# A fused attention and MLP kernel: exps of q and k moved behind the logits' exp, VectorE's steps spread between matmuls, logits spaced differently

## Chip, cores and metric

The kernel runs on 1 core of one Trainium2 chip. The metric is the device time in microseconds (us) of one execution; each figure for a kernel is the median over repeated runs. A core has several engines, each with its own queue of instructions that it executes in order: TensorE (PE in the profile, its weight loads PEld), VectorE (DVE), ScalarE (ACT), GpSimd (POOL) and SyncE (SP, which here only issues DMAs). They wait for one another through semaphores. Matmul results go to PSUM, which has 8 banks; SBUF is the other on-chip memory.

## What is computed

From `x` (2048 tokens of width 1024, bfloat16) the layer-normalised `xn` is formed, and the output is `x + A(xn) + B(xn)`. `B` is an MLP over the token axis. `A` is attention of 32 heads of 32 columns, over 4 segments of 512 tokens, with a memory that each segment leaves for the next:

```python
phi = lambda t: jnp.where(t > 0, t + 1.0, jnp.exp(t))
g = _sigmoid(beta).reshape(1, H, 1, 1)
for s in range(N):
    logits = jnp.einsum('bhqd,bhkd->bhqk', qs, ks) * scale + mask
    p = _softmax(logits, axis=-1)
    a_dot = jnp.einsum('bhqk,bhkd->bhqd', p, vs)
    pq = phi(qs)
    num = jnp.einsum('bhld,bhde->bhle', pq, M)
    den = jnp.einsum('bhld,bhd->bhl', pq, z)[..., None] + 1e-06
    o = g * (num / den) + (1.0 - g) * a_dot
    pk = phi(ks)
    M = M + jnp.einsum('bhld,bhle->bhde', pk, vs)
    z = z + jnp.einsum('bhld->bhd', pk)
return o @ wo
```

The mask is causal within a segment, and `phi(t)` is computed as `max(t + 1, min(exp(t), 1))`.

## The kernel before

The MLP runs first, up to about 352 us, then attention. All instructions are issued by one Python program, in the order in which its functions are called; each engine executes its own in that order, and a small framework adds the semaphore waits. Nothing reorders them afterwards.

**Units.** Attention is cut into 32 units, one for each group of four heads in each segment: unit `u` is segment `u // 8`, group `u % 8`. The loop of `attention` (L1313) runs over the units.

**Dense work.** The projections are jobs of 8 matmuls of 128x512 each, kept in the queue `self.jobs` and run in order by `dense(n)`, which issues the next `n` of these matmuls, across job borders. A job uses PSUM bank 6 or 7, in turn, and when its eighth matmul has been issued its `end` issues what empties the bank: a ScalarE copy into `qT` (`q_job`) or `vA` (`v_job`), a VectorE copy into `kT` (`k_job`), or a VectorE addition into `fin` (`wo_job`, the output projection). The bank can be written again once that is done. In unit `u` the queue holds the output projections planned for it, one v job up to unit 27, and the q and k jobs of unit `u + 2` up to unit 29. So units 10 to 25 and 27 have four jobs (32 matmuls, in the order wo, v, q, k), unit 30 has two (wo, wo), unit 31 three (wo), and the others three: v, q, k in units 0 to 9 and 26, wo, q, k in units 28 and 29.

**Logits.** `logits(u, step)` multiplies q and k of four heads at once into banks 0 to 3 and then issues one ScalarE exp over all four banks into `pT`, and one GpSimd select for each diagonal block, which zeroes what the mask excludes. Step 0 is the first block of rows of k, step 1 the second and the fourth; step 2, the third, is done for two units together in the even one. The next logits can be written when the exp has read the banks.

**Weighing.** `weigh(u - 1, part)` multiplies `pT` with v, phi(q) with the memory, and in part 2, in segments 0 to 2, phi(k) with v for the memory's update. Parts 0 and 2 write bank 4, part 1 bank 5. After each part VectorE copies the result into `ost`; after part 2 it also updates the memory (`MZ`, `MZbf`, L1254 to L1258). Part 2 can start only when the copy of part 0 has emptied bank 4.

**Mixing and phi.** `combine(u - 1)` is VectorE's mixing of the two attention results: three small operations for the scales (`srec`, L1282 to L1284), the product `prod` (L1285), and the addition into `o_s` (L1289). In segment 0 there is no memory and it has two small operations and one product. `phi_q` and `phi_k` are two VectorE operations each (L1070 and L1072), on an exp that ScalarE has put into one of the four buffers `etmp` before; that exp is issued by the `end` of the q or k job. `k_transpose` sends phi(k) through a transposing DMA into `pk`; `o_transpose_dma` does so for `o_s`. In the first four units of segments 0 to 2 a chunk of `x` for the next segment is loaded (`xn_load`), scaled on VectorE (`xn_scale`) and transposed (`xn_transpose`).

**Order in a unit.** `cut` divides the unit's matmuls among five stretches by shares. An even unit issues logits 0, 6 dense matmuls, weighing parts 0 and 1, 2 dense, weighing part 2, phi of k, the scaling of x, 4 dense, logits 1, combine, phi of q, 12 dense, logits 2, and 8 dense (shares of 32; with 24 they are 4, 2, 3, 9 and 6). An odd unit issues 4 dense, logits 0, 6 dense, weighing parts 0 and 1, 2 dense, weighing part 2, phi of k, the scaling, 6 dense, logits 1, combine, phi of q, and 14 dense. After the last unit `tail` finishes the last segment's output.

In the profile, every matmul has line L198, that of a helper, so one tells them by the names of their tiles: `ps_all<-qT,kT` are logits; `vA,pT`, `MZbf,pqT` and `vA,pk` are weighing; `xnT,wq`, `xnT,wk`, `wv,xnT` and `wo,oT` are dense.

Of the kernel before, what the change touches and what calls it, by code (L numbers as in the profile page):

```python
# [6 lines left out]
ACT = mybir.ActivationFunctionType  # L7
# [12 lines left out]
P = 128  # L20
# [364 lines left out]
class _Kernel:  # L385
# [678 lines left out]


    def phi(self, dst, R_dst, src, R_src, k, u):

        fw = self.fw
        et, R_et, mt = self.etmp[2 * (u % 2) + k], self.R_etmp[2 * (u % 2) + k], self.mtmp[k]
        fw.op("dve", lambda e: e.tensor_scalar(mt[:], et[:], 1.0, None, op0=ALU.min),  # L1070
              reads=[R_et], writes=[self.R_mtmp[k]])
        fw.op("dve", lambda e: e.scalar_tensor_tensor(dst, src, 1.0, mt[:], op0=ALU.add, op1=ALU.max),  # L1072
              reads=[R_src, self.R_mtmp[k]], writes=[R_dst])
# [16 lines left out]
    def q_job(self, u):  # L1090
        def end(b):
            fw, k = self.fw, u % 3
            fw.op("act", lambda e: e.activation(self.qT[k][:], self.bank(b), ACT.Copy),  # L1093
                  reads=[self.R_bank[b]], writes=[self.R_qT[k]])
            if u >= N_GRP:
                fw.op("act", lambda e: e.activation(self.etmp[2 * (u % 2)][:], self.qT[k][:], ACT.Exp),  # L1096
                      reads=[self.R_qT[k]], writes=[self.R_etmp[2 * (u % 2)]])
        return self.proj_job(self.wq_ring, u, end)

    def k_job(self, u):  # L1100
        def end(b):
            fw, k = self.fw, u % 3
            fw.op("dve", lambda e: e.tensor_copy(self.kT[k][:], self.bank(b)),  # L1103
                  reads=[self.R_bank[b]], writes=[self.R_kT[k]])
            if u // N_GRP < N_SEG - 1:
                fw.op("act", lambda e: e.activation(self.etmp[2 * (u % 2) + 1][:], self.kT[k][:], ACT.Exp),  # L1106
                      reads=[self.R_kT[k]], writes=[self.R_etmp[2 * (u % 2) + 1]])
        return self.proj_job(self.wk_ring, u, end)
# [151 lines left out]

    def combine(self, u):
        fw = self.fw
        s, g, o = u // N_GRP, u % N_GRP, u % 2
        ost, R_ost = self.ost[o], self.R_ost[o]
        rec, R_rec = self.srec[:, o, :], self.R_srec[o]
        os, R_os = self.o_s[o], self.R_os[o]
        if s == 0:
# [3 lines left out]
            fw.op("dve", lambda e: e.tensor_tensor(rv, rv, self.gate[:, g, None, 0, :].to_broadcast([P, 4, 4]),  # L1271
                                                   op=ALU.mult), reads=[R_rec, self.R_gate], writes=[R_rec])
            fw.op("dve", lambda e: e.tensor_tensor(os[:].rearrange("p q (r d) -> p q r d", d=D_HEAD),
                                                   v[:, :, 0, :, 0:D_HEAD],
                                                   rv.unsqueeze(3).to_broadcast([P, 4, 4, D_HEAD]), op=ALU.mult),
                  reads=R_ost + [R_rec], writes=[R_os])
            return
        sums = ost[:, :, D_HEAD].rearrange("p (q a) -> p q a", q=4)
        rv = rec.rearrange("p (q a) -> p q a", q=4)
        e8 = self.eps8[:].rearrange("p k r -> p (k r)")[:, None, :].to_broadcast([P, 4, 8])  # L1280
        g8 = self.gate[:, g, :, :].rearrange("p k r -> p (k r)")[:, None, :].to_broadcast([P, 4, 8])
        fw.op("dve", lambda e: e.tensor_tensor(rv, sums, e8, op=ALU.add), reads=R_ost + [self.R_eps8], writes=[R_rec])  # L1282
        fw.op("dve", lambda e: e.reciprocal(rec, rec), reads=[R_rec], writes=[R_rec])
        fw.op("dve", lambda e: e.tensor_tensor(rv, rv, g8, op=ALU.mult), reads=[R_rec, self.R_gate], writes=[R_rec])  # L1284
        fw.op("dve", lambda e: e.tensor_tensor(self.prod[:], ost[:, :, 0:D_HEAD],  # L1285
                                               rec.unsqueeze(2).to_broadcast([P, 32, D_HEAD]), op=ALU.mult),
              reads=R_ost + [R_rec], writes=[self.R_prod])
        pv = self.prod[:].rearrange("p (q k r) d -> p q k (r d)", q=4, k=2)
        fw.op("dve", lambda e: e.tensor_tensor(os[:], pv[:, :, 0, :], pv[:, :, 1, :], op=ALU.add),  # L1289
              reads=[self.R_prod], writes=[R_os])  # L1290

# [15 lines left out]

    WO_FIRST = 10

# [9 lines left out]
    def attention(self):  # L1319
        self.jobs, self.turn = deque(), 0  # L1320
        self.wo_plan = {}
        for s in range(N_SEG - 1):
# [3 lines left out]
        self.jobs.extend([self.q_job(0), self.k_job(0)] + [self.v_job(0, c) for c in range(4)])  # L1326
        self.dense(16)
        self.phi_k(0)
        self.k_transpose(0)
# [4 lines left out]
        for u in range(N_UNIT):  # L1334
# [17 lines left out]
            self.dense(cuts[1] if not even else 0)  # L1352
            if u:
# [32 lines left out]
    def tail(self):  # L1386
# [30 lines left out]
        self.weigh(u, 2)  # L1417
        self.combine(u)
        product(3, 0, 6)
# [38 lines left out]
```

## Time and profile before

| what | value |
|---|---|
| median of 11 runs | 666.29 us (665.48 to 668.38) |
| device time of the profiled execution | 667.29 us |
| its span (first to last instruction) | 665.5 us |
| granted TensorE clock | 1.00 throughout |

Stretches of the profiled execution, from the view that gives busy time by window:

| stretch, us | what | long | TensorE busy | VectorE | ScalarE | GpSimd |
|---|---|---|---|---|---|---|
| 0 to 365.5 | MLP, first projections | 365.5 | 361.89 | 198.65 | 76.12 | 53.01 |
| 365.5 to 442.7 | units 0 to 9 | 77.2 | 75.39 | 45.19 | 63.58 | 25.43 |
| 442.7 to 598.1 | units 10 to 25 | 155.4 | 152.69 | 131.96 | 109.17 | 49.64 |
| 598.1 to 649.9 | units 26 to 31 | 51.8 | 48.55 | 37.80 | 33.45 | 16.76 |
| 649.9 to 665.5 | tail | 15.6 | 12.93 | 8.88 | 0.60 | 0.00 |

A row of a timeline gives the start in us from the span's start, the busy time, the engine, the line, the operation with its tiles, the number of instructions merged into the row, and in brackets the idle time before it with what ended it. A row of the chain of waits gives start, length, and the engine with its tile and line. A matmul's busy time includes its way through the array, so rows of TensorE overlap, and a TensorE that is busy all the time can still issue matmuls later than it could. DMA transfers land, in the median, 2.3 us after issue for `pk`, 3.7 us for `oT`, 3.2 us for `xnT`, and 3.4 and 3.9 us for a group's `wq` and `wk`.

### The profile page before, as it was taken

The numbers are of one execution on the slowest core, as the hardware profiler recorded it, in microseconds if no ns is written. First come the engines' busy times: TensorE is split into PE (matmuls) and PEld (weight loads), VectorE is DVE, ScalarE is ACT, GpSimd is POOL, SyncE is SP. The second block draws the span as 40 slices with busy tenths as digits, with TensorE's granted clock in tenths as the row PEclk, the third lists the DMA queues.
The fourth block names the chain that finished last, engine by engine and source line by source line (L and its number), as shares of the span: only waits on it lengthen the run. The fifth ranks groups of instructions, "written<-read, shape, count | busy, mean of one in ns | idle before, by whom it ended". The sixth has DMA issues, their size and how long they took to land.

```text
span 665.5 us, 11075 instructions
## 1 busy us (share of the span) xinstructions
PE 651.4 (98%) x4622; PEld 301.6 (45%) x4622; DVE 422.5 (63%) x789; ACT 282.9 (43%) x305; POOL 144.8 (22%) x181
## 2 busy tenths in 40 slices
PE   8999999999999999999999999989999999999988
PEld 3444444444444444444444444444444444444434
DVE  6965676665653554335442455588889988776775
ACT  7442232322300000000012888866767666767750
POOL 2500000000020222202250333333332233323330
PEclk9999999999999999999999999999999999999999
DMA  9704242242637644665185686586446765434225
GB/s 309 198 0 128 64 123 67 68 123 64 178 122 205 159 142 126 175 175 142 67 222 176 162 177 118 112 158 153 111 120 125 167 146 120 119 88 77 75 75 134
DMA packets 187241, 87.64 MB, mean 132 GB/s; under 512 B 116024, under 2 KB 174392, under 8 KB 187192
## 3 DMA queue, kind: packets, MB, share of 16 engines
q1 hardware_dynamic: 187048, 86.91, 51.9%
q8 instruction: 36, 0.59, 0.4%
q14 instruction: 13, 0.11, 0.1%
q10 hardware_dynamic: 144, 0.03, 0.0%
HBM read 67.13 MB, written 8.39 MB: 113 GB/s over the span
## 4 chain that ended last, share of the span: by engine, by line
PE 81%; ACT 9%; DVE 7%; issue 1%; DMA 1%; SPq 0%; DVEq 0%
PE ps_all L198 81%; ACT pT L1198 6%; ACT etmp L1096 1%; DVE prod L1285 1%; ACT qT L1093 1%; DVE mtmp L1070 1%; DMA xin<-in_A_x_dram 1%; DVE o_s L1289 1%; DVE kT L1103 1%; ACT etmp L1106 1%; DVE gate L558 1%; DVE fin L1406 1%; DVE ost L1248 1%; DVE mtmp L1072 1%; DVE pqT L1072 0%
## 5 line engine op out<-in xcount | busy, mean ns | idle before, releaser
L1198 ACT ACTIVATE pT<-ps_all 128x2048 bf16<-128x2048 f32 x80 | 149.6, 1869 | 29.6 <-PE ps_all L198 29.5
L1202 POOL TENSOR_SCALAR_AFFINE_SELECT pT<-pT 128x512 bf16<-128x512 bf16 x128 | 91.8, 734 | 209.5 <-ACT pT L1198 209.5
L690 DVE TENSOR_TENSOR part<-ps_all,part 128x512 f32<-128x512 f32 x76 | 55.5, 730 | 117.1 <-PE ps_all L198 116.2
L926 POOL TENSOR_TENSOR part<-part,stg 128x512 f32<-128x512 f32 x24 | 33.0, 1402 | 265.0 <-DVE part L690 248.1
L695 ACT ACTIVATE part<-ps_all 128x512 f32<-128x512 f32 x20 | 11.9, 597 | 149.0 <-PE ps_all L198 149.0
L742 ACT ACTIVATE g<-part,b1c 128x512 f16<-128x512 f32 x36 | 26.0, 722 | 98.8 <-DVE part L690 98.8
L198 PE MATMUL ps_all<-wv,xnT 128*128 128x512 bf16 x256 | 66.8, 379 | 0.0
L198 PE MATMUL ps_all<-wo,oT 128*128 128x512 bf16 (+2 forms) x272 | 64.2, 367 | 1.4 <-DVE fin L1146 1.3
L198 PE MATMUL ps_all<-xnT,wq 128*128 128x512 bf16 x256 | 65.2, 380 | 0.0
L1248 DVE CAST ost<-ps_all 128x396 bf16<-128x396 f32 (+2 forms) x96 | 42.8, 474 | 33.3 <-PE ps_all L198 32.5
L198 PE MATMUL ps_all<-xnT,wk 128*128 128x512 bf16 x256 | 61.8, 380 | 0.0
L198 PE MATMUL ps_all<-g,sum 128*128 128x512 f16 x224 | 51.0, 379 | 0.8 <-DVE part L690 0.8
L198 PEld LDWEIGHTS ps_all<-vA,pT 128*128 128x128 bf16 x1280 | 42.2, 96 | 19.7 <-DVE ost L1248 10.5
L198 PE MATMUL ps_all<-g,w2s 128*128 128x512 f16 x224 | 51.0, 379 | 0.0
L198 PE MATMUL ps_all<-gT,sum 128*128 128x512 f16 x224 | 49.7, 379 | 0.0
L198 PE MATMUL ps_all<-vA,pT 128*128 128x33 bf16 x1280 | 45.2, 178 | 1.6 <-DVE ost L1248 1.6
L198 PE MATMUL ps_all<-h,sum 128*128 128x512 f16 x192 | 45.2, 379 | 0.0
L198 PE MATMUL ps_all<-h,w1s 128*128 128x512 f16 x192 | 44.9, 379 | 0.0
L198 PE MATMUL ps_all<-hT,sum 128*128 128x512 f16 x192 | 43.6, 379 | 0.0
L198 PEld LDWEIGHTS ps_all<-xnT,wk 128*128 128x128 bf16 x256 | 23.8, 98 | 29.9 <-issue 3.2
L198 PE MATMUL ps_all<-qT,kT 32*128 32x384 bf16 (+3 forms) x512 | 31.7, 301 | 4.8 <-ACT pT L1198 3.9
L198 PEld LDWEIGHTS ps_all<-wo,oT 128*128 128x128 bf16 x272 | 23.2, 97 | 27.5 <-issue 5.8
(98 smaller groups left out, 817.9 us busy)
## 6 DMA issues: line engine op xcount, KB each, us to landing
w2s<-in_B_w_dram SPq DMA_DIRECT2D x8, 1792.0 KB, 8.5
w1s<-in_B_w_dram SPq DMA_DIRECT2D x12, 1024.0 KB, 5.6
wq<-in_A_wq_dram SPq DMA_DIRECT2D x32, 256.0 KB, 3.4
wk<-in_A_wk_dram SPq DMA_DIRECT2D x32, 256.0 KB, 3.9
stg<-in_A_x_dram SPq DMA_DIRECT2D x16, 256.0 KB, 2.9
xs<-in_A_x_dram SPq DMA_DIRECT2D x16, 256.0 KB, 4.2
out_dram<-stg SPq DMA_DIRECT2D x16, 256.0 KB, 2.8
fin<-out_dram SPq DMA_DIRECT2D x16, 256.0 KB, 3.1
```

Of the source, the lines that this page charges most:

```text
L198: ins = self.nc.tensor.matmul(*args, **kwargs)
L558: fw.op("dve", lambda e: e.tensor_copy(self.gate[:, :, 1, :], gv), reads=[self.R_gcol, self.R_gate], writes=[self.R_gate])
L690: self.fw.op("dve", lambda e: e.tensor_tensor(self.tmp[dst][:], self.bank(b), self.tmp[src][:], op=ALU.add), reads=[self.R_bank[b], self.R ...
L695: self.fw.op("act", lambda e: e.activation(self.tmp[dst][:], self.bank(b), ACT.Copy), reads=[self.R_bank[b]], writes=[self.R_tmp[dst]])
L742: self.fw.op("act", lambda e: e.activation(self.gB[f % 2][half][:, f // 2, :], src, ACT.Gelu_apprx_tanh, bias=self.b1c[:, f:f + 1], scale= ...
L926: fw.op("pool", lambda e: e.tensor_tensor(self.tmp[t][:], self.tmp[t][:], self.stg[k][:, 512 * half:512 * half + 512], op=ALU.add), reads= ...
L1070: fw.op("dve", lambda e: e.tensor_scalar(mt[:], et[:], 1.0, None, op0=ALU.min), reads=[R_et], writes=[self.R_mtmp[k]])
L1072: fw.op("dve", lambda e: e.scalar_tensor_tensor(dst, src, 1.0, mt[:], op0=ALU.add, op1=ALU.max), reads=[R_src, self.R_mtmp[k]], writes=[R_ ...
L1093: fw.op("act", lambda e: e.activation(self.qT[k][:], self.bank(b), ACT.Copy), reads=[self.R_bank[b]], writes=[self.R_qT[k]])
L1198: fw.op("act", lambda e: e.activation(dst, src, ACT.Exp, scale=SCALE), reads=self.R_bank[0:4], writes=[R[v % 2][kb] for v, kb, _ in blocks ...
L1202: fw.op("pool", lambda e: e.affine_select(d, d, pattern=[[0, 4], [1, P]], compare_op=ALU.is_ge, fill=0.0, base=0, channel_multiplier=-1), ...
L1248: fw.op("dve", lambda e: e.tensor_copy(dst, src), reads=[self.R_bank[b]], writes=[self.R_ost[o][part]])
```

## The change

Three things are changed in the attention phase; nothing is computed differently.

- The exps of q and k are no longer issued at the end of their jobs. They are noted in `self.exps`, and `late_exps`, called at the end of `logits`, issues them behind that logits' exp and its selects.
- `combine` returns its work as a list of steps (two in segment 0, else four, with the product in two halves), and these steps, phi of q, phi of k with its transpose, and the scaling with its transpose are put into a queue `self.side`. `dense` takes one step from it after every three matmuls. Phi of q is now that of unit `u` in unit `u`, not that of `u + 1`. What is left at the unit's end is issued there.
- The shares are now 5, 1, 3, 15, 8 in an even unit (logits 0, 5 dense, weighing parts 0 and 1, 1 dense, part 2, 3 dense, logits 1, 15 dense, logits 2, 8 dense) and 7, 4, 1, 4, 16 in an odd one (7 dense, logits 0, 4 dense, parts 0 and 1, 1 dense, part 2, 4 dense, logits 1, 16 dense).

```diff
+    def late_exps(self):
+        for k, src, R, u in self.exps:
+            n = 2 * (u % 2) + k
+            assert self.in_etmp[n] is None, (n, u, self.in_etmp)
+            self.in_etmp[n] = u
+            self.fw.op("act", lambda e: e.activation(self.etmp[n][:], src[:], ACT.Exp), reads=[R], writes=[self.R_etmp[n]])
+        self.exps = []
...
             if u >= N_GRP:
-                fw.op("act", lambda e: e.activation(self.etmp[2 * (u % 2)][:], self.qT[k][:], ACT.Exp),
-                      reads=[self.R_qT[k]], writes=[self.R_etmp[2 * (u % 2)]])
+                self.exps.append((0, self.qT[k], self.R_qT[k], u))
...
             if u // N_GRP < N_SEG - 1:
-                fw.op("act", lambda e: e.activation(self.etmp[2 * (u % 2) + 1][:], self.kT[k][:], ACT.Exp),
-                      reads=[self.R_kT[k]], writes=[self.R_etmp[2 * (u % 2) + 1]])
+                self.exps.append((1, self.kT[k], self.R_kT[k], u))
...
             stop = min(at + n, 8)
+            if self.side:
+                stop = min(stop, at + max(1, self.SIDE_EVERY - self.since))
...
             if stop == 8:
                 end(b)
                 self.jobs.popleft()
+            self.since += stop - at
+            if self.side and self.since >= self.SIDE_EVERY:
+                self.side.popleft()()
+                self.since = 0
...
+        self.late_exps()
...
+        def products(half):
+            n = slice(16 * half, 16 * half + 16)
+            fw.op("dve", lambda e: e.tensor_tensor(self.prod[:, n, :], ost[:, n, 0:D_HEAD],
+                                                   rec[:, n].unsqueeze(2).to_broadcast([P, 16, D_HEAD]), op=ALU.mult),
+                  reads=R_ost + [R_rec, self.R_prod], writes=[self.R_prod])
...
+        if s == 0:
+            return [scales_first, products_first]
+        return [scales, lambda: products(0), lambda: products(1), add]
...
-    WO_FIRST = 10
+    SIDE_EVERY = 3
...
+            cuts = self.cut(total, (5, 1, 3, 15, 8) if even else (7, 4, 1, 4, 16))
             if even:
-                cuts = (self.cut(total, (6, 2, 4, 12, 8)))
                 self.logits(u, 0)
             else:
-                cuts = (self.cut(total, (4, 6, 2, 6, 14)))
-            self.dense(cuts[0])
-            if not even:
+                self.dense(cuts[0])
                 self.logits(u, 0)
             if u > 1:
                 self.o_transpose_dma(u - 2)
-            self.dense(cuts[1] if not even else 0)
+            self.dense(cuts[0] if even else cuts[1])
             if u:
                 self.weigh(u - 1, 0)
                 self.weigh(u - 1, 1)
             self.dense(cuts[1] if even else cuts[2])
             if u:
                 self.weigh(u - 1, 2)
+                steps = self.combine(u - 1)
+                self.side.append(steps.pop(0))
+            if N_GRP <= u:
+                self.side.append(lambda: self.phi_q(u))
+            if u:
+                self.side.extend(steps)
             if u + 1 < N_UNIT:
-                self.phi_k(u + 1)
-                self.k_transpose(u + 1)
+                self.side.append(lambda: (self.phi_k(u + 1), self.k_transpose(u + 1)))
             if xn:
-                self.xn_scale(c)
+                self.side.append(lambda: (self.xn_scale(c), self.xn_transpose(c)))
             self.dense(cuts[2] if even else cuts[3])
             self.logits(u, 1)
-            if u:
-                self.combine(u - 1)
-            self.phi_q(u + 1)
-            if xn:
-                self.xn_transpose(c)
             if even:
                 self.dense(cuts[3])
                 self.logits(u, 2)
             self.dense(100)
+            while self.side:
+                self.side.popleft()()
```

In the changed program's order on VectorE, a unit of segments 1 to 3 has the three copies into `ost`, the memory's update, the scales, phi of q, both halves of `prod`, the addition into `o_s`, phi of k, the scaling of x where there is one, and the copy into `kT`; an even unit's `fin` stands right behind the scales, an odd unit's ahead of the copies. Before, `fin` of an even unit stood between the second and the third copy.

More of the change, by code (lines that the diff above doesn't have):

```diff
@@ L1063, in before_attention @@
                       reads=[self.R_diag], writes=[self.R_diag])
+    def late_exps(self):
[5 more added lines that the diff above has]
+        self.exps = []
     def phi(self, dst, R_dst, src, R_src, k, u):
         fw = self.fw
+        assert self.in_etmp[2 * (u % 2) + k] == u
+        self.in_etmp[2 * (u % 2) + k] = None
         et, R_et, mt = self.etmp[2 * (u % 2) + k], self.R_etmp[2 * (u % 2) + k], self.mtmp[k]
@@ L1266, in combine, with scales_first @@
         os, R_os = self.o_s[o], self.R_os[o]
-        if s == 0:
+        def scales_first():
             v = ost[:].rearrange("p (q k r) x -> p q k r x", q=4, k=2)
@@ L1272, in combine, with products_first @@
                                                    op=ALU.mult), reads=[R_rec, self.R_gate], writes=[R_rec])
+        def products_first():
+            v = ost[:].rearrange("p (q k r) x -> p q k r x", q=4, k=2)
+            rv = rec[:, 0:16].rearrange("p (q r) -> p q r", q=4)
             fw.op("dve", lambda e: e.tensor_tensor(os[:].rearrange("p q (r d) -> p q r d", d=D_HEAD),
@@ L1276, in combine @@
                   reads=R_ost + [R_rec], writes=[R_os])
[L1277 to L1288, printed above, removed]
@@ L1289, in combine, with scales @@
-        fw.op("dve", lambda e: e.tensor_tensor(os[:], pv[:, :, 0, :], pv[:, :, 1, :], op=ALU.add),
-              reads=[self.R_prod], writes=[R_os])
+        def scales():
+            sums = ost[:, :, D_HEAD].rearrange("p (q a) -> p q a", q=4)
+            rv = rec.rearrange("p (q a) -> p q a", q=4)
+            e8 = self.eps8[:].rearrange("p k r -> p (k r)")[:, None, :].to_broadcast([P, 4, 8])
+            g8 = self.gate[:, g, :, :].rearrange("p k r -> p (k r)")[:, None, :].to_broadcast([P, 4, 8])
+            fw.op("dve", lambda e: e.tensor_tensor(rv, sums, e8, op=ALU.add), reads=R_ost + [self.R_eps8], writes=[R_rec])
+            fw.op("dve", lambda e: e.reciprocal(rec, rec), reads=[R_rec], writes=[R_rec])
+            fw.op("dve", lambda e: e.tensor_tensor(rv, rv, g8, op=ALU.mult), reads=[R_rec, self.R_gate], writes=[R_rec])
@@ new lines, in products, with add @@
+        def products(half):
[3 more added lines that the diff above has]
+                  reads=R_ost + [R_rec, self.R_prod], writes=[self.R_prod])
+        def add():
+            pv = self.prod[:].rearrange("p (q k r) d -> p q k (r d)", q=4, k=2)
+            fw.op("dve", lambda e: e.tensor_tensor(os[:], pv[:, :, 0, :], pv[:, :, 1, :], op=ALU.add),
+                  reads=[self.R_prod], writes=[R_os])
@@ L1320, in attention @@
         self.jobs, self.turn = deque(), 0
+        self.side, self.since = deque(), 0
+        self.exps, self.in_etmp = [], [None] * 4
         self.wo_plan = {}
@@ L1327, in attention @@
         self.dense(16)
+        self.late_exps()
         self.phi_k(0)
@@ L1417, in tail @@
         self.weigh(u, 2)
-        self.combine(u)
+        for step in self.combine(u):
+            step()
         product(3, 0, 6)
```

## The prediction, as put on record before the result

> **What bounds the kernel now.** I read the page's busy line first, then the waits of TensorE over the attention phase (390 to 646 us), then the chain of waits and the timeline of one pair of units.
>
> ```profile
> PE 651.4 (98%) x4622; PEld 301.6 (45%) x4622; DVE 422.5 (63%) x789; ACT 282.9 (43%) x305; POOL 144.8 (22%) x181
> ```
>
> TensorE is nearly always at work, so the change can only take away, or add, moments in which TensorE waits. Which those are:
>
> ```profile
> PE ps_all L198 <- ACT pT L1198: 3.1, 9, 0.6
> PE ps_all L198 <- DVE ost L1248: 1.6, 3, 1.0
> PE ps_all L198 <- DVE fin L1146: 1.3, 1, 1.3
> ```
>
> This counts only time in which the array had drained. A better measure is the start of each matmul against the one before: where nothing waits, dense matmuls follow each other at 0.216 us, a logits step costs 0.10 more on entry and 0.33 until the next dense one, weighing matmuls follow at 0.025 (33 columns) and 0.057 (132). Whatever the timeline shows above that I call a stall. Over all units it adds up to 11.0 us: 6.05 before logits (waiting for the exp of the logits before), 3.5 before the third weighing group (waiting for VectorE's copy of the first), and 1.4 at a dense matmul behind `fin` (637.7 us). No edit of this kind can win more than this.
>
> The chain shows where the logits' stalls come from:
>
> ```profile
> 464.40 0.69 DVE pqT L1072
> 465.09 0.61 DVE kT L1103
> ...
> 465.73 0.63 ACT etmp L1106
> 466.36 1.77 ACT pT L1198
> 468.13 0.05 issue
> 468.18 3.11 PE ps_all L198 x20
> ```
>
> The exp of kT waits for VectorE's kT copy, and the logits' exp is queued behind it on ScalarE, so TensorE's next logits start only at 468.18, a stall of 0.28.
>
> **The change, part by part.** Positions count dense matmuls within a unit; units 10 to 25 and 27 have 32, unit 30 has 16, the others 24.
>
> *1. The exps of q and k go behind the next logits' exp, logits come evenly.* In a 32 unit the logits are now 15 or 16 dense matmuls apart (or 9 with the weighing), at least 3.6 us; ScalarE needs 0.45 from the logits' start to its exp and 1.88 for it, and banks are free 2.39 after the logits. The late exps (0.63 each) fill what is left, so these stalls go: 2.57 in units 10 to 25, 1.07 in units 1 to 9, 1.25 of 1.50 at the end (unit 30 has 8 dense matmuls between two logits, 8 x 0.216 + 0.33 + 0.10 = 2.16 against 2.39, and keeps 0.25). Unit 0 had 0.90, as its exp stood behind an exp of kT; now its second logits come after 7 dense matmuls instead of 9 and 0.42 is left: 0.48 won. Together -5.4.
>
> *2. `fin` between the steps.* At 637.7 TensorE waited 1.42 for a `fin` queued behind prod, o_s and both phi steps. In the new order it stands behind phi of q and ahead of prod. Counted from unit 30's first logits: third group at 0.33 + 2 x 0.216 + 1.16 (part 3) = 1.92, its copy 0.67 later, 0.47 until the scales, these 0.85, phi 0.93 to 1.36, fin 0.69, release 0.06: done at 5.6 to 6.0. The bank is wanted after 13 more dense matmuls and two logits, 1.92 + 0.46 + 2.81 + 0.86 + 0.25 = 6.3. -1.4.
>
> *3. One dense matmul between second and third weighing group instead of two.* Both orders leave bank 4 to be copied by VectorE before the third group may write it:
>
> ```profile
> 561.75 0.26 PE L198 MATMUL ps_all<-vA,pT 128*128 128x33 bf16 x4
> ...
> 562.30 1.05 DVE L1248 CAST ost<-ps_all 128x396 bf16<-128x396 f32 x2 [0.22 <-PE ps_all L198]
> ...
> 562.53 0.59 PE L198 MATMUL ps_all<-wo,oT 128*128 128x512 bf16 x2
> ...
> 562.96 0.56 PE L198 MATMUL ps_all<-vA,pT 128*128 128x33 bf16 x16
> ```
>
> The copy is 0.56 of that 1.05 and ends at 562.86; 0.06 later the group may start, at 562.92. Two dense matmuls carry TensorE to 562.96, just enough; one carries it to 562.75: a stall of 0.17. Where one matmul stands already, the trace has it:
>
> ```profile
> 390.22 0.76 PE L198 MATMUL ps_all<-vA,pT 128*128 128x33 bf16 x24
> 390.71 0.64 DVE L1248 CAST ost<-ps_all 128x264 bf16<-128x264 f32 x2 [1.52 <-PE ps_all L198]
> 390.82 0.38 PE L198 MATMUL ps_all<-xnT,wq 128*128 128x512 bf16 x1
> 391.20 0.57 PE L198 MATMUL ps_all<-vA,pT 128*128 128x33 bf16 x16
> ```
>
> 0.38 between the last two starts, 0.16 over the pitch. Units 10 to 25: 16 x 0.17 = +2.7. In even 24 units the shares round to no matmul at all: the copy is done 0.98 after 390.22's like, TensorE is there after 0.61, stall 0.37 instead of 0.03, for units 2, 4, 6, 8: +1.35. Units 26 to 31: 0.38, 0.17, 0.38, 0.44, 0.17, 0.43 (29 and 31 as now, with a `fin` ahead of the copy) against 1.07 now: +0.9. Together +5.0. The cover is work that TensorE does anyway; nothing else hides this wait.
>
> *4. VectorE's steps.* Between the weighing of an odd unit and of the next even one TensorE has one dense matmul fewer (25 for 26, 0.22 us), and VectorE has one instruction more: prod in halves, each as long as the other product of 512 elements (0.69, plus 0.035 as the second half and the add each wait for the one before), 1.46 for 1.26, +0.20. In the trace VectorE was 0.22 early for the copy in unit 22 (the idle time in the row above); it will be 0.20 late. In even units after an odd one that scales xs (0.46 more) it was 0.17 late (a stall of 0.11 behind the cover of 0.05) and will be 0.59. Unit 10, behind a short unit 9, was 1.22 late (stall 1.17) and will be 1.67. That delay adds to the wait of part 3: 3 x 0.20 (units 14, 16, 22) + 3 x 0.59 (12, 18, 20) + 1.67 = 4.05, against 1.5 now in these units: +2.55. Unknown here is how the masks on GpSimd fall: its select holds up the VectorE instruction that it meets, o_s 0.42 to 0.74, the min 0.28 to 0.72, prod once 1.22 to 1.59. Two selects per odd unit now cost 0.74. If they meet nothing, all but unit 10 are on time and this part is -0.6; if they meet one instruction more (0.4 x 7), +5.4. I take the same 0.74, as two selects still follow the same logits' exp while prod and the add run.
>
> [...]
>
> *5. `fin` of an even 32 unit moves behind ost, MZ, MZbf and the scales.* From the third group's start (562.96): third copy 0.91 later, then 0.87 until the next instruction, scales 0.85, fin 0.69, release 0.06: 3.38. The q projection wants that bank at 0.70 + 10 x 0.216 + 0.41 = 3.27. +0.11, 8 units: +0.9. Bounds: nothing, if VectorE runs 0.11 quicker; 2.1 if MZbf meets a select each time (0.30 to 0.45).
>
> *6. The v copy in even 24 units falls behind a logits' exp.* v ends at 8, the second logits now stand at 7, not 9, so vA's copy is queued behind that exp, and the k projection needs v's bank again at 16.
>
> ```profile
> 468.62 1.88 ACT L1198 ACTIVATE pT<-ps_all 128x2048 bf16<-128x2048 f32 x1 [0.51 <-PE ps_all L198]
> 470.40 0.59 ACT L1131 ACTIVATE vA<-ps_all 128x512 bf16<-128x512 f32 x1
> ```
>
> Such a copy starts 1.78 after its exp: 0.45 + 1.78 + 0.59 + 0.06 = 2.88 after the logits. TensorE reaches k after 0.33 + 9 x 0.216 = 2.27. Stall 0.61, in units 0, 2, 4, 6, 8, 26: +3.7.
>
> *At nothing:* the splits of dense groups (wo runs keep 0.216 across the present ones); transposes of pk and xnT, later on SP's queue and ahead of wq or wk there: a pk lands 2.3 us after issue and is wanted a unit later, a wq 3.4 us and is wanted two units later. `o_transpose_dma` waits for o_s, which is done some 2 us before the unit ends. Without that cover a late weight load would stall TensorE for its lateness.
>
> **Sum.** -5.4 - 1.4 + 5.0 + 2.55 + 0.9 + 3.7 = +5.3. The profiled execution took 667.29 for a span of 665.5, 1.0 above the median of 666.29; the same difference on the median gives 671.6 (span 670.8). Parts 4 and 5 at their low ends give +1.3 (667.6), at their high ends +9.4 (675.7).
>
> **The rivals.**
> - *Forecast, slower by waits on banks (0.68):* 671.6, from 667.6 to 675.7.
> - *Faster (0.12):* the ScalarE queue was what fed VectorE's lateness too. For it: the chain runs from VectorE through the two exps into TensorE, and VectorE is idle 1.6 us ahead of `fin` in odd units. If VectorE then has bank 4 free in time, parts 3, 4 and 5 cost nothing beyond the present 3.5: -5.4 - 1.4 + 3.7 = -3.1, 663.2. Against it: the copy starts only when the first group ends, and 0.38 at 390.82 is that with an idle VectorE. It decides once the 0.17 is under 0.05.
> - *VectorE becomes the bound (0.12):* units 10 to 23 run at 17.4 of 20 us busy; if each select blocks fully and kT's copy misses its bank as well (it ends within 0.1 of the v projection's start in odd units), a pair loses another 0.6, 7 pairs: +4.2 over the forecast, 675.8. Against it: in odd units VectorE waits 0.5 for the third group.
> - *Even trade (0.08):* parts 3 and 1 cancel (+5.0, -5.4), part 6 doesn't appear because the exp starts early enough, part 5 is at 0: 666.29 - 5.4 - 1.4 + 5.0 + 2.55 = 667.0. Against it: the exp needs its logits, which are 9 dense matmuls ahead of k, less than the exp itself with its 0.45.
>
> Under 0.2% (1.3 us) is taken for no change. Faster 0.12, same 0.08, slower 0.80. The range, 666.8 to 675.7, is the forecast's own with the fourth case added: outside lie the second and about half of the third, 0.2.
>
> **What would show it.** In the changed profile: no waits of TensorE for pT in units 10 to 25; starts 0.38 apart at the single dense matmul of odd units from 10 on, 0.4 to 0.9 in even ones; a wait of 0.6 before the k projection of units 2 to 8, on vA; 0.1 before q on `fin`; nothing at 637.7. Wrong if waits on ost do not grow, or if the pairs from unit 12 on become shorter than 19.1 us.

## The result and the profile after

The changed kernel takes 673.18 us (median of 12 runs, 671.49 to 675.17). The kernel before, run again beside it, takes 666.61 (47 runs). The ratio is 1.0097, with a 95% interval from 1.0084 to 1.0110: slower by about 1%. The profiled execution of the changed kernel took 672.89 for a span of 671.2.

The page's busy line and, further down on it, the engines' shares of the chain that ended last, then the same line of shares for the kernel before:

```profile
PE 654.8 (98%) x4622; PEld 301.9 (45%) x4622; DVE 422.6 (63%) x813; ACT 279.8 (42%) x305; POOL 148.2 (22%) x181
...
PE 88%; DVE 7%; ACT 3%; issue 1%; DMA 1%; SPq 0%; DVEq 0%
```

```profile
PE 81%; ACT 9%; DVE 7%; issue 1%; DMA 1%; SPq 0%; DVEq 0%
```

ScalarE's share of the chain fell from 9% to 3%: the late exps did what they were to do. The time went elsewhere, and the waits of TensorE over attention, from 362 to 652 us (us in total, times, longest), say where:

```profile
PE ps_all L198 <- DVE ost L1263: 5.3, 12, 1.7
PE ps_all L198 <- ACT vA L1139: 3.1, 6, 0.5
PE ps_all L198 <- ACT pT L1212: 0.5, 2, 0.4
```

In the kernel before, this row of the same stretch stands beside the prediction's rows for `ost` and `fin`:

```profile
PE ps_all L198 <- ACT pT L1198: 3.9, 10, 0.8
```

Waits for `pT` fell from 3.9 us to 0.5 (the 3.1 of the prediction leaves out unit 0). Waits for `ost`, the copy that empties bank 4, grew from 1.6 to 5.3, and waits for `vA`, which before had none, are 3.1.

By the measure of the prediction (start of each matmul against the one before), stalls were 11.4 us before and are 18.3 now. The prediction had 11.0 before: it left out 0.28 at a `fin` in unit 31 and some small ones. Attention alone, from unit 0's first logits to the end of the span, grew from 300.01 to 307.16 (+7.2). The spans differ by 5.7 only, because unit 0's first logits came 1.5 us earlier in this execution. That start varies by 3 us over the profiles below, whose MLP is the same, so I compare attention alone where I compare profiles. The two profiles of the changed kernel differ by 0.4 in it, so a difference of that size between two runs says little.

The timeline of TensorE in an even unit of 32 matmuls (unit 18):

```profile
527.62 0.46 PE L198 MATMUL ps_all<-vA,pT 128*128 128x33 bf16 x12
...
527.98 0.38 PE L198 MATMUL ps_all<-wo,oT 128*128 128x512 bf16 x1
528.81 0.57 PE L198 MATMUL ps_all<-vA,pT 128*128 128x33 bf16 x16 [0.45 <-DVE ost L1263]
```

One dense matmul stands between the weighing groups, and the third group starts 0.83 after it, 0.61 over the pitch of 0.216. TensorE and ScalarE in unit 4, which has 24 matmuls:

```profile
399.03 0.40 PE L198 MATMUL ps_all<-qT,kT 32*128 32x384 bf16 x8
...
402.00 0.59 PE L198 MATMUL ps_all<-xnT,wk 128*128 128x512 bf16 x2 [0.52 <-ACT vA L1139]
```

```profile
399.48 1.88 ACT L1212 ACTIVATE pT<-ps_all 128x2048 bf16<-128x2048 f32 x1 [1.26 <-PE ps_all L198]
401.26 0.59 ACT L1139 ACTIVATE vA<-ps_all 128x512 bf16<-128x512 f32 x1
```

The copy of v is queued behind the exp of the logits of 399.03 and ends only at 401.85; the k projection is due at 401.3 and starts at 402.00. That is a stall of 0.68.

Something that the prediction has no step for happens in unit 10. TensorE waits 1.72 us there with nothing in the array, until 448.95, and 0.92 us later the granted clock falls. First the timeline, then the busy time by window (length, then PE, PEld, VectorE, ScalarE and GpSimd, then the granted clock, the DMA share and GB/s):

```profile
446.85 0.38 PE L198 MATMUL ps_all<-wo,oT 128*128 128x512 bf16 x1
448.95 0.57 PE L198 MATMUL ps_all<-vA,pT 128*128 128x33 bf16 x16 [1.72 <-DVE ost L1263]
```

```profile
448.90:450.00 1.10, 1.05 (x23) 0.94 (x24) 0.61 (x2) 0.00 (x0) 0.00 (x0) 0.94 0.52 116
450.00:453.00 3.00, 3.00 (x15) 0.73 (x14) 2.86 (x10) 1.49 (x1) 0.00 (x0) 0.50 0.81 188
453.00:454.00 1.00, 1.00 (x5) 0.45 (x4) 0.97 (x3) 0.39 (x1) 0.54 (x1) 0.86 0.42 92
454.00:456.00 2.00, 2.00 (x17) 0.73 (x16) 1.93 (x4) 0.84 (x2) 1.20 (x2) 1.00 0.00 0
```

The clock is 0.50 for 3.41 us (449.87 to 453.28). Dense matmuls follow each other at 0.427 in this stretch instead of 0.216, which costs 1.5 us: from the third group's start to the k projection, unit 10 takes 1.54 longer than unit 18.

### The profile page after: what moved, and what is told of

It is laid out like the page before. It is cut to its first block, busy times and chain, and to the rows that moved or that the text cites. A ratio compares the mean times of both kernels' runs of the same rounds, so it can differ in the third digit from the quotient of the medians.

```text
span 671.2 us, 11120 instructions
## 1 busy us (share of the span) xinstructions
PE 654.8 (98%) x4622; PEld 301.9 (45%) x4622; DVE 422.6 (63%) x813; ACT 279.8 (42%) x305; POOL 148.2 (22%) x181
## 4 chain that ended last, share of the span: by engine, by line
PE 88%; DVE 7%; ACT 3%; issue 1%; DMA 1%; SPq 0%; DVEq 0%
PE ps_all L198 88%; ACT pT L1212 2%; DVE ost L1263 1%; DVE prod L1310 1%; DMA xin<-in_A_x_dram 1%; DVE gate L558 1%; DVE fin L1440 1%; DVE mtmp L1080 1%; ACT vA L1139 0%; DVE pqT L1082 0%; DVE mtmp L1082 0%; DVE fin L1154 0%; DVE kT L1112 0%; DVE xs L986 0%; DVE srec L1305 0%
## 5 line engine op out<-in xcount | busy, mean ns | idle before, releaser
L1216 POOL TENSOR_SCALAR_AFFINE_SELECT pT<-pT 128x512 bf16<-128x512 bf16 x128 | 95.2, 761 | 212.7 <-ACT pT L1212 212.7
L695 ACT ACTIVATE part<-ps_all 128x512 f32<-128x512 f32 x20 | 11.9, 597 | 149.0 <-PE ps_all L198 149.0
L198 PE MATMUL ps_all<-wv,xnT 128*128 128x512 bf16 x256 | 68.2, 385 | 0.0
L198 PE MATMUL ps_all<-wo,oT 128*128 128x512 bf16 (+2 forms) x272 | 65.6, 368 | 1.0 <-DVE fin L1154 1.0
L198 PE MATMUL ps_all<-xnT,wq 128*128 128x512 bf16 x256 | 62.5, 379 | 0.0
L1310 DVE TENSOR_TENSOR prod<-ost,srec 128x512 bf16<-128x512 bf16 x48 | 40.1, 835 | 0.9
L1112 DVE CAST kT<-ps_all 128x512 bf16<-128x512 f32 x32 | 22.0, 687 | 26.9 <-PE ps_all L198 26.9
```

What stands on the lines that cost most here:

```text
L198: ins = self.nc.tensor.matmul(*args, **kwargs)
L695: self.fw.op("act", lambda e: e.activation(self.tmp[dst][:], self.bank(b), ACT.Copy), reads=[self.R_bank[b]], writes=[self.R_tmp[dst]])
L1310: fw.op("dve", lambda e: e.tensor_tensor(self.prod[:, n, :], ost[:, n, 0:D_HEAD], rec[:, n].unsqueeze(2).to_broadcast([P, 16, D_HEAD]), op ...
```

## The experiments

The theory is the prediction's, with the clock added: the shares cost time by waits on banks (bank 4 before the third weighing group, v's bank before k), the late exps gain about 5 us, and the steps change little. The main rival puts the loss on VectorE or on the order of its work: the steps, or prod in halves. Attention alone is in us from the profile of each run; medians are compared with the kernel before in the same rounds.

| run | median | before | ratio, 95% interval | attention alone |
|---|---|---|---|---|
| changed kernel | 673.18 | 666.61 | 1.0097 [1.0084, 1.0110] | 307.16 (before: 300.01) |
| old_cuts | 660.05 | 666.8 | 0.9897 [0.9875, 0.9920] | 295.30 |
| exps_only | 662.34 | 666.8 | 0.9930 [0.9906, 0.9953] | 296.05 |
| cuts_only | 680.83 | 666.8 | 1.0211 [1.0183, 1.0239] | 315.14 |
| side_only | 665.26 | 666.8 | 0.9978 [0.9958, 0.9997] | 299.46 |
| two_matmuls | 666.58 | 667.29 | 0.9982 [0.9967, 0.9996] | 300.88 |
| v_first | 667.94 | 667.29 | 1.0018 [0.9999, 1.0036] | 301.78 |
| prod_whole | 669.09 | 667.29 | 1.0032 [1.0017, 1.0048] | 304.19 |
| unit10 | 670.13 | 667.29 | 1.0047 [1.0029, 1.0065] | 304.15 |
| best | 657.09 | 666.36 | 0.9856 [0.9832, 0.9880] | 291.05 |
| after_again | 673.49 | 666.36 | 1.0089 [1.0062, 1.0116] | 307.59 |
| best_tail | 655.35 | 667.21 | 0.9816 [0.9802, 0.9831] | 290.69 |
| ten_alone | 666.95 | 667.21 | 1.0004 [0.9986, 1.0023] | 301.18 |

### The parts alone

**old_cuts**: the changed kernel with the old shares.

```diff
-            cuts = self.cut(total, (5, 1, 3, 15, 8) if even else (7, 4, 1, 4, 16))
+            cuts = self.cut(total, (6, 2, 4, 12, 8) if even else (4, 6, 2, 6, 14))
```

> The changed kernel with the old shares (6, 2, 4, 12, 8 and 4, 6, 2, 6, 14); late exps and steps stay. Bank theory (the new shares cost 5.0 + 3.7 of waits on banks 4, 6 and 7, the rest of the change wins): the third weighing group waits 0.1 or less in most units, no wait for vA, logits' stalls stay away: 660.5 us, between 659 and 662.5. VectorE theory (the steps and the halved prod overload VectorE, the shares matter little): 670 or more.

660.05: the late exps and the steps without the new shares are faster than the kernel before by 1%. Its waits of TensorE over attention:

```profile
PE ps_all L198 <- DVE ost L1263: 1.7, 4, 1.0
PE ps_all L198 <- ACT pT L1212: 1.3, 3, 0.6
PE ps_all L198 <- DVE fin L1154: 1.0, 1, 1.0
```

No wait for `vA`, four for `ost`, and few for `pT`: even with logits at their old places the late exps remove most of those. The new shares were not needed for the gain that they were combined with.

**exps_only**: the kernel before with `self.exps` and `late_exps` alone.

```diff
-                fw.op("act", lambda e: e.activation(self.etmp[2 * (u % 2) + 1][:], self.kT[k][:], ACT.Exp),
-                      reads=[self.R_kT[k]], writes=[self.R_etmp[2 * (u % 2) + 1]])
+                self.exps.append((1, self.kT[k], self.R_kT[k], u))
```

> The kernel before with the late exps alone: no steps between matmuls, old shares, prod in one piece. Bank theory: nearly all stalls before logits go (5.4 us of 6.05; the one in unit 30 and the wait for fin there stay): 661.5 us, between 660.5 and 663. If VectorE's lateness was behind the logits' stalls anyway: 665 or more.

662.34, and attention is 4.0 shorter than before. By the starts, the stalls before logits shrink by 4.9 us; what is left of them is 0.40 in unit 0 and 0.65 in unit 30. The prediction had 5.4 for part 1, together with the even spacing, so the exps alone bring nine tenths of it. Attention won less than 4.9 mainly because the stall for `ost` in unit 10 grew from 1.18 to 1.84.

**cuts_only**: the kernel before with the new shares alone.

> The kernel before with the new shares alone: exps at the end of their jobs, combine in one piece. Bank theory: the waits of parts 3 and 6 (5.0 and 4.1) come in full and 2 to 4 us of the logits' stalls go by the spacing alone: 673 to 675.5 us. VectorE theory (the steps did it): 664 to 667.

680.83, and attention 15.1 longer: far worse than any theory had it. Its waits:

```profile
PE ps_all L198 <- DVE ost L1248: 8.2, 24, 1.3
PE ps_all L198 <- ACT pT L1198: 4.3, 9, 1.3
PE ps_all L198 <- DVE fin L1146: 3.3, 2, 2.0
PE ps_all L198 <- ACT vA L1131: 3.1, 6, 0.5
```

The `ost` and `vA` waits are there as in the changed kernel, so they belong to the shares. (Some of the 24 waits for `ost` are not waits: records of matmuls are missing from this trace too, as explained under v_first.) The stalls before logits did not go by the spacing, as the bank theory had it: about 5 us of them are left. What I had not counted is what the old order of VectorE does under them. Its timeline before the q projection at 535.28, which starts 1.46 late:

```profile
531.80 0.28 DVE L1070 TENSOR_SCALAR mtmp<-etmp 128x512 bf16<-128x512 bf16 x1
532.12 1.04 DVE L1072 SCALAR_TENSOR_TENSOR mtmp<-kT,mtmp 128x512 bf16<-128x512 bf16 x1
533.98 0.55 DVE L986 TENSOR_SCALAR xs<-xs,ln_mv,ln_rs 128x1024 bf16<-128x1024 bf16 x1 [0.83 <-DMA xs<-in_A_x_dram]
534.45 0.68 DVE L1146 TENSOR_TENSOR fin<-ps_all,fin 128x512 bf16<-128x512 f32 x1
```

`fin` is queued behind phi of k and behind a scaling that itself waits 0.83 for its DMA. Without the late exps, an exp of kT also still stands ahead of each logits' exp (0.4 to 0.5 before step 1 in units 10 to 22).

**side_only**: the changed kernel with the old shares and the exps issued at once, so that of the change only the steps are left.

```diff
                 self.exps.append((1, self.kT[k], self.R_kT[k], u))
+                self.late_exps()
```

> The changed kernel with old shares and each exp issued at once at the end of its job: only the steps between matmuls and the halved prod are new. Bank theory: 1.4 won at unit 30's fin, some 0.2 lost per even unit from 10 on through VectorE: 666 us, between 665 and 668. VectorE theory: 670 or more.

665.26: the steps alone are worth 0.5 us of attention. With the old shares the late exps bring 4.0 without the steps and 4.2 with them, so the two parts add up. The loss is then the shares': +11.9 us on the changed kernel with old shares (307.16 against 295.30), of which the clock is 1.5. The rival that puts it on the steps falls.

### The shares taken apart

**two_matmuls**: two dense matmuls between second and third weighing group.

```diff
-            cuts = self.cut(total, (5, 1, 3, 15, 8) if even else (7, 4, 1, 4, 16))
+            cuts = self.cut(total, (5, 2, 2, 15, 8) if even else (7, 4, 2, 3, 16))
```

> The changed kernel with two dense matmuls instead of one between the second and third weighing group (shares 5, 2, 2, 15, 8 and 7, 4, 2, 3, 16). Bank theory: the waits on ost shrink by 0.2 in every unit, 5.7 us in all, but in the even units from 10 to 24 the q projection then reaches the bank of fin one matmul sooner and waits 0.25 there, so these give back 1.5: 669.1 us, between 668 and 670.2. If those waits are not what costs the time: 672 or more.

666.58. The stalls of 0.19 in odd units and of 0.18 in units 14, 16, 22 and 24 shrink to 0.04 or nothing. Attention is 6.3 shorter than the changed kernel's; 1.5 of this is the halved clock, which this profile does not have although its wait in unit 10 is even longer (1.77). The rest, 4.8, is a little over the 4.1 expected, but not for the reason given: the waits on `ost` give less than 5.7, and the waits of 0.25 before the q projection, which were to give back 1.5, are not there. In units 10 to 25, stalls of 0.49 to 0.50 are left in units 12, 18 and 20 and one of 1.93 in unit 10, where VectorE is late.

**v_first**: in even units of 24, shares that end v after the second logits.

```diff
+            if even and total == 24:
+                cuts = (4, 0, 4, 10, 6)
```

> The changed kernel with one matmul moved in even units of 24 (shares 4, 0, 4, 10, 6), so that v ends before the second logits and vA's copy goes ahead of their exp. Bank theory: six waits of 0.68 on vA go, 0.07 comes at each third logits: 669.5 us, between 668.5 and 670.5. Otherwise 672 or more.

667.94, with attention 5.4 shorter, 3.9 without the clock (expected 3.7). The six waits for `vA` are gone, in exchange for two shorter ones on `pT` in unit 0. TensorE's waits:

```profile
PE ps_all L198 <- DVE ost L1263: 8.7, 24, 1.6
...
PE ps_all L198 <- DVE fin L1154: 1.0, 1, 1.0
PE ps_all L198 <- ACT pT L1212: 0.3, 2, 0.2
```

The `ost` row counts 24 waits here and 12 in the changed kernel. The twelve more are no waits: matmul records are missing from this trace. Its page has 54 matmuls fewer than weight loads, where the changed kernel's page has 4622 of both:

```profile
PE 647.9 (97%) x4568; PEld 302.8 (45%) x4622; DVE 420.5 (63%) x813; ACT 279.6 (42%) x305; POOL 148.2 (22%) x181
```

In each of the twelve places the one dense matmul between the weighing groups has its weight load but no record, so the array looks empty while it runs. Seven more of the profiles below and above (old_cuts, exps_only, cuts_only, side_only, two_matmuls, prod_whole, unit10) lack 53 to 55 records as well; their counts of waits, and a start that follows a missing matmul, must be read with that in mind.

**prod_whole**: prod in one instruction, still as a step.

```diff
-            n = slice(16 * half, 16 * half + 16)
+            n = slice(0, 32)
...
-        return [scales, lambda: products(0), lambda: products(1), add]
+        return [scales, lambda: products(0), add]
```

> The changed kernel with prod in one instruction. In its trace the halves take 0.84 on average, 1.67 for the two against 1.26. Bank theory: only the four even units in which VectorE is late (10, 12, 18, 20) gain, 0.2 to 0.4 each: 672 us, between 671 and 672.8, and unit 10 waits 1.5 to 1.7. VectorE theory (VectorE is the bound in all units from 10 to 23): 668 or less.

669.09. Unit 18 again, now with a stall of 0.42 instead of 0.61:

```profile
526.24 0.38 PE L198 MATMUL ps_all<-wo,oT 128*128 128x512 bf16 x1
526.88 0.57 PE L198 MATMUL ps_all<-vA,pT 128*128 128x33 bf16 x16 [0.26 <-DVE ost L1263]
```

Units 12, 18 and 20 win 0.19 each, unit 10 wins 0.38, and `fin` at the tail 0.50: 1.5 together, and attention is 3.0 shorter with the clock's 1.5.

The medians of two_matmuls, v_first and prod_whole all lie under the ranges expected for them. The halved clock accounts for 1.5 of that: the expectations started from the changed kernel's median, which holds it, and these three profiles don't have it. In prod_whole 0.5 more is the tail's `fin`. What is left, up to 1 us in two_matmuls and prod_whole, has no name.

**unit10**: shares of its own for unit 10, so that TensorE has ten dense matmuls while VectorE is late.

```diff
+            if u == 10:
+                cuts = (5, 10, 1, 8, 8)
```

> The changed kernel with ten dense matmuls instead of one between the second and third weighing group of unit 10 alone (shares 5, 10, 1, 8, 8 there). The wait of 1.88 is then covered. If the drop of TensorE's clock to 0.5 for 3.4 us right behind it (450 us) comes of that wait, it goes too: 669.9 us, between 669 and 671, clock 1.00 in units 9 to 12. If the drop has another cause it stays: 671.3.

670.13, with attention 3.0 shorter. The stall of 1.88 becomes two of 0.36 (before logits) and 0.08, and the clock stays at 1.0 in the profile. The mean clock is 0.997 or lower in one of ten runs, against ten of twelve of the changed kernel.

### A version that beats both

**best**: the changed kernel with old shares, prod whole, shares of their own where old_cuts still had stalls, and one tail product moved behind the weighing.

```diff
+    CUTS = {0: (4, 2, 3, 11, 4), 1: (5, 4, 2, 4, 9), 3: (3, 4, 2, 5, 10), 5: (3, 4, 2, 5, 10), 7: (3, 4, 2, 5, 10),
+            9: (3, 4, 2, 5, 10), 10: (6, 7, 1, 10, 8), 29: (3, 4, 3, 4, 10), 30: (2, 2, 0, 9, 3), 31: (6, 3, 3, 2, 10)}
...
         product(0, 0, 6)
-        product(1, 0, 6)
         self.weigh(u, 0)
         self.weigh(u, 1)
-        product(2, 0, 6)
+        product(1, 0, 6)
         self.weigh(u, 2)
...
+        product(2, 0, 6)
```

> The changed kernel with the old shares, prod in one instruction, shares of their own in ten units (0, 1, 3, 5, 7, 9, 10, 29, 30, 31), and in the tail one product ahead of the last weighing instead of two. Banks and VectorE's lateness: the stalls left in the kernel with the old shares go, namely 4 x 0.16 (odd units 3 to 9), 1.12 (unit 10), 3 x 0.18 (units 12, 18, 20, by prod in one piece), 2 x 0.43 (units 29 and 31, a fin ahead of the copy), 0.65 + 0.43 - 0.22 (logits of units 30 and 31), 0.39 (unit 0) and 1.2 (the third fin of unit 31 ahead of the tail's second product): 5.6 less than 660.05, so 654.5; 656.5 if the last chain of DMAs takes back half of the end's part. Other theory, that the kernel is near a floor set by VectorE's own work, so that a stall taken away in one unit comes back in the next: 658 to 660.

657.09: between the two theories. No wait for `ost` or `pT` is left. But the tail's wait for `fin` only moved with its product (1.01 where 1.21 was), a `fin` in unit 30 now costs 0.48, and kT's copy 0.39 in unit 10. So attention won 4.25 on old_cuts and not 5.6, and the start before attention was 1.2 longer in this profile.

**best_tail**: the second and third product of the tail change places, so that the one within the weighing writes a bank without a `fin`.

> The kernel of the run before, with the tail's second and third product changed places: the product between the weighing groups writes a bank that no fin reads. Banks theory: the stall of 1.01 ahead of that product goes, as the fin that it waited for has another 2 us until its bank is wanted: 656.1 (655.5 to 656.6). If the end is set by the last combine and its DMAs and not by TensorE there, nothing changes: 657.1.

655.35 against 667.21, 1.8% faster than the kernel before, and just under the range expected. What is left of TensorE's waits over attention:

```profile
PE ps_all L198 <- DVE fin L1154: 0.3, 1, 0.3
PE ps_all L198 <- DVE kT L1112: 0.2, 1, 0.2
PE ps_all L198 <- DMA oT<-o_s: 0.2, 1, 0.2
```

The wait of 1.01 is gone, but 0.20 for `ost` and 0.38 for the transposed output come in its place, and attention is only 0.36 shorter than in `best`. The two medians come from different rounds, so their difference of 1.7 is not put down to this edit.

### The clock

**after_again**: the changed kernel once more, in other rounds.

> The changed kernel once more, on the chip and in the rounds of the other run. If the halved clock belongs to the kernel's wait in unit 10, most runs show a mean granted clock of 0.997 or less and the median is 672 to 674. If it belonged to the chip or the moment of the first measurement, most runs show 1.0 and the median is 671.5 or less.

673.49; the profile has the halved clock again, behind the same wait (from 450.31, for 3.41 us). Three of its six runs have a mean clock of 0.997, which is half and not most of them as expected; they take 674.4 in the median and the other three 670.4.

**ten_alone**: two_matmuls with one dense matmul in unit 10.

```diff
+            if u == 10:
+                cuts = (5, 1, 3, 15, 8)
```

> The kernel with two matmuls between the weighing groups, but with one in unit 10, as in the changed kernel, so that TensorE's wait there stands behind one dense matmul and not two. If the halved clock comes where the share of work around the wait is low enough, it shows behind unit 10 in most runs (a clock of 0.997 or less), and the median is 1.0 to 2.0 above the 666.6 of its parent: 667.6 to 668.6. If what decides is something else than this matmul, most runs stay at 1.0 and the median at 666.4 to 667.0 (the wait becomes longer by what the matmul took).

666.95, and four of twelve runs at 0.997: no more than the kernel before, which has such a clock in 23 of 73 runs, and two_matmuls itself (three of ten). The wait in unit 10 is longer than in the changed kernel, behind one matmul as there, and this profile shows no drop:

```profile
445.22 0.38 PE L198 MATMUL ps_all<-wo,oT 128*128 128x512 bf16 x1
447.47 0.57 PE L198 MATMUL ps_all<-vA,pT 128*128 128x33 bf16 x16 [1.87 <-DVE ost L1263]
```

So one matmul fewer ahead of the wait does not bring the drop in most runs. The section on the hardware takes this up.

## Why the prediction was right, and where it was off

The forecast, slower by waits on banks, is what happened, by the places that it named. The median is 1.6 us above the predicted 671.6, and the sum lacked one term of about that size, the halved clock. The two runs of the changed kernel with a mean clock of 1.0 took 671.49 and 671.78, the other ten 673.6 in the median. That the rest comes out so near is partly luck: the parts are off by -0.9 to +0.8, and these errors cancel to +0.2. By its parts, from the starts in the two profiles:

| part | predicted | measured |
|---|---|---|
| 1. stalls before logits | -5.4 | -5.4 |
| 2. `fin` late in units 30 and 31 | -1.4 | -0.6 |
| 3 and 4 in units 0 to 9 | +1.35 | +1.7 |
| 3 and 4 in units 10 to 25 | +5.25 | +4.4 |
| 3 in units 26 to 31 | +0.9 | +1.0 |
| 5. `fin` before q | +0.9 | +0.3 |
| 6. `vA` | +3.7 | +4.1 |
| halved clock behind unit 10 | none | +1.5 |
| sum | +5.3 | +7.0 |

The sum of stalls over all (18.3 less 11.4) is +6.9 and attention itself +7.2; 0.3 stays without a name.

- *Part 1* was right to a tenth, its two remainders too (0.44 in unit 0 for 0.42, 0.22 in unit 30 for 0.25). The runs add that it hardly needed the shares: the exps alone bring 4.9 of it.
- *Part 2* named the stall at 637.7, and it is gone, but the part stopped one unit early. In unit 31 the third `fin` now stands behind the halves of prod and o_s. VectorE and TensorE there in the changed kernel:

```profile
651.10 1.72 DVE L1310 TENSOR_TENSOR prod<-ost,srec 128x512 bf16<-128x512 bf16 x2
652.85 0.73 DVE L1316 TENSOR_TENSOR o_s<-prod 128x512 bf16<-128x512 bf16 x1
653.51 0.68 DVE L1154 TENSOR_TENSOR fin<-ps_all,fin 128x512 bf16<-128x512 f32 x1
```

```profile
650.76 2.54 PE L198 MATMUL ps_all<-wo,oT 128*128 128x512 bf16 x11
654.25 1.47 PE L198 MATMUL ps_all<-wo,oT 128*128 128x512 bf16 x6 [0.95 <-DVE fin L1154]
```

  TensorE stalls 1.11 where it stalled 0.28. I counted the new order once and not for every `fin` that passes through it.
- *Part 3*: one dense matmul was predicted to cost 0.17 and costs 0.186 in each odd unit from 11 on; no matmul was predicted at 0.37 and costs 0.467 in units 2 to 8. The 0.10 is in the release: the third group starts 0.148 after its copy's end in these units, and 0.058 after it in those with a dense matmul between. The missing matmul is not the whole reason, as units 26 and 28 have none either and start after 0.058; what decides is not shown.
- *Part 4*: unit 10 waits 1.88 (predicted 1.84). Units 12, 18 and 20 have 0.61 for 0.76. Units 14, 16, 22 have 0.18 for 0.37: VectorE is on time there. From the third copy in unit 21 to the first in unit 22 its work takes 6.62; before it could have done so in 6.55, as one instruction starts 0.06 before the one ahead has ended its busy time, so its lead was 0.28 and not 0.22. The halves add 0.18, and the new order of scales and phi takes 0.11 off, which I had left at nothing. With 0.21 from the missing dense matmul, the lead is just used up. Where VectorE is late the halves cost what was predicted: prod_whole gives back 0.19 in each such unit. The 0.74 for the masks, taken over from the kernel before, held too: in unit 21 they add 0.31 to o_s and 0.43 to the min. In the kernel before, the o_s at 559.38 meets a select that ends at 559.84, 0.46 later, and takes 0.31 longer; the min at 560.04 meets one that ends at 560.61, 0.57 later, and takes 0.43 longer. Each loses less than the rest of the select that it meets.
- *Part 5* was too high: 0.045 in seven units for 0.11 in eight.
- *Part 6* has its mechanism and place right, and 0.68 for 0.61: here too the release takes 0.145, not the 0.06 of the sum.
- *The missing term*: the prediction took the granted clock as it was, 1.00 throughout, and lengthened the wait in unit 10 from 1.17 to 1.84 without a term for a drop of the clock behind it, which both profiles of the changed kernel show (0.5 for 3.41 us).

The rivals: the faster one was to decide once the 0.17 is under 0.05, and it is 0.186. The even trade needed `vA`'s wait to stay out, and it is there six times. VectorE did not become the bound: the waits are for one copy, at one place, and two_matmuls ends those of the units in which VectorE is on time without touching VectorE's work. Of units 10 to 25 only 10, 12, 18 and 20 wait because VectorE is late. That a select blocks fully, that rival's condition, no run shows, nor the 0.6 a pair put on it: the two meetings above cost 0.31 and 0.43.

## What to carry to other kernels

When work is spaced anew, list for each PSUM bank who empties it and who wants it next, under the new order: even logits cost more on the weighing's and v's banks than they won, and the gain came almost wholly from the order on ScalarE's queue (4.0 to 4.2 us, the steps 0.5). A part of a change that wins should be tried without the parts beside it: here two of three parts are worth 1%, and the third turned them into a loss. A queue that works in order must be checked for each item behind a moved step, up to the last unit and the tail.

## What the runs showed of the hardware

The clock's drop was not expected. In the changed kernel's profile it lasts 3.41 us (449.87 to 453.28), in that of after_again as long (450.31 to 453.72). These are TensorE's waits in unit 10 in each profile in which they are over 1.3 us:

| profile | idle, us | clock behind it |
|---|---|---|
| changed kernel | 1.72 | 0.5 for 3.41 us |
| after_again | 1.72 | 0.5 for 3.41 us |
| ten_alone | 1.87 | 1.0 |
| two_matmuls | 1.77 | 1.0 |
| exps_only | 1.68 | 1.0 |
| v_first | 1.60 | 1.0 |
| prod_whole | 1.34 | 1.0 |
| cuts_only | 1.34 | 1.0 |

In these eight the length of the wait alone does not decide: behind 1.72 the clock falls in both profiles, behind 1.77 and 1.87 it stays at 1.0. The same kind of wait stands at the start of the kernel, for `h` (the normalised input of the MLP). The matmul behind it in exps_only, then in unit10:

```profile
7.09 0.38 PE L198 MATMUL ps_all<-h,w1early 128*128 128x512 f16 x1 [2.14 <-DVE h L628]
```

```profile
7.01 0.38 PE L198 MATMUL ps_all<-h,w1early 128*128 128x512 f16 x1 [1.71 <-DVE h L628]
```

Behind the wait of 2.14 the clock is halved from 7.45 to 10.87. Side_only has a drop there too (a mean clock of 0.55 from 8 to 10 us and of 0.60 from 10 to 12). Behind the 1.71 in unit10 and a wait of 1.5 in old_cuts the clock stays at 1.0. It also does in cuts_only, which has a wait of 2.00 for `fin` in unit 28:

```profile
634.02 0.38 PE L198 MATMUL ps_all<-xnT,wk 128*128 128x512 bf16 x1 [2.00 <-DVE fin L1146]
```

What decides beside the length is not shown. All this was read after the fact, and no run was made to test it. The drops at the start also show that a run's mean clock does not tell where a drop was: the profiled execution of exps_only has 0.997, with its drop at the start, and that of the changed kernel has 0.997, with its drop in unit 10. The kernel before has such runs too. So the 13 of 18 runs of the changed kernel and the 4 of 12 of ten_alone may count drops at the start along with those in unit 10, and why the two differ stays open.
